# Seven products of halves instead of eight in the first matrix product of an attention and feed-forward kernel

## The chip, the cores and the metric

The kernel runs on one core of one Trainium2 chip. The metric is device microseconds of one execution, as the median of several runs. The rows of the profile come from one profiled execution; its times are in microseconds (us) from the span's start unless they say ns.

## What is computed

The inputs are q, k and v of shape (8 batches, 8 heads, 576 positions, 64), and two weights, w_in (512 x 2048) and w_out (2048 x 512). Attention is done within chunks of 64 positions, and its output goes through a feed-forward layer:

```python
scores = scale * np.matmul(q_c, k_c.transpose(0, 1, 2, 4, 3))
attn = softmax(scores)
x = np.matmul(attn, v_c)        # as 4608 tokens x 512
h = x @ w_in                    # first product, 512 -> 2048
g = np.where(h > 0.0, h, np.exp(np.minimum(h, 0.0)) - 1.0)
out = g @ w_out                 # second product, 2048 -> 512
```

All of it is in float32, the weights arrive as float64 and are turned into float32 on the chip.

## The kernel before

The 4608 tokens are worked through in 9 blocks of 512 (`TB`). The 2048 hidden features are 16 slices of 128 (index `f`), and the 512 model features are 4 slices of 128 (`kt`). A matrix is held as a sum of two float32r parts, hi and lo, and each product is made of three matmuls: hi by hi, hi by lo, lo by hi (`three`, L395). One matmul has a 128 x 128 weight operand and 512 moving columns.

For each block and each f, `hidden` (L400) makes h, 128 features x 512 tokens, with 4 x 3 matmuls that accumulate in one PSUM bank. `elu` (L408) has five operations on it: ScalarE takes the negative part (L411) and its exponential (L412), VectorE combines it with h from PSUM (L414), ScalarE casts the result to the hi part `ghi` (L419), VectorE subtracts to get `glo` (L422). `project` (L425) adds g's slice, one f later (`LAG`), to four PSUM banks `o`, one for each 128 tokens, with 4 x 3 matmuls of 512 columns. After the last f of a block `store` (L431) copies the four banks out and writes them to DRAM. All hi and lo parts of both weights stay in SBUF: `weights` (L79) holds for each half of f the tiles `wi_hi`, `wi_lo` (4096 words for each partition and tile) and `wo_hi`, `wo_lo`. In the first block they are split as they arrive.

Attention for the next block runs beside this, one tile of 128 tokens for four f (`attention_tile`, L339). Its steps are, in order: two transposes of q and k on VectorE (L275, L278), eight score matmuls (L349, two instructions each), maximum and subtraction on VectorE (L355, L369), the exponential on ScalarE (L373), the sum and the scaling on VectorE (L375 to L308), eight transfers between partitions on the DMA queue of SyncE (L320), two transposes on VectorE (L325), eight matmuls with v (L333), and a copy to `xf` on ScalarE (L384). At a block's end `split_next` (L535) makes `xhi` and `xlo` of `xf`.

PE, ScalarE, VectorE and SyncE each run their instructions in the order in which the program issues them. That order is written out by hand: a line of letters for each f (`SECOND_BLOCK` L467, `LATER` L473). H is `hidden`, P is `project` of the slice before, e is one step of `elu`, a and n are one step of the present and the next attention tile, X is `split_next`:

```python
    LATER = (
        "a a H e e e e P",
        "a H e e e e P",
        "n n H e e e e P",
        "n a a n H n X P e e e e",
    )
```

GpSimd sets constants at the start and does nothing later. SyncE issues all transfers.

Of the kernel before, what the change touches and what calls it, by code (L numbers as in the profile page):

```python
# [15 lines left out]
ALU = mybir.AluOpType  # L16
# [4 lines left out]
def kernel(  # L21
# [14 lines left out]

    nc = tc.nc
# [14 lines left out]
    Q = 32  # L52
    LAG = 1
# [13 lines left out]
    ps_h = ctx.enter_context(tc.tile_pool(name="ps_h", bufs=2, space=bass.MemoryType.PSUM))  # L67

# [158 lines left out]
    def load_tokens(n0: int):  # L227
# [4 lines left out]
        qk = stp.tile([P, STAGE], F32, name="st")  # L232
# [162 lines left out]
    def three(ps, a_hi, a_lo, b_hi, b_lo, start, stop):  # L395
        nc.tensor.matmul(ps, lhsT=a_hi, rhs=b_hi, start=start, stop=False)  # L396
        nc.tensor.matmul(ps, lhsT=a_hi, rhs=b_lo, start=False, stop=False)  # L397
        nc.tensor.matmul(ps, lhsT=a_lo, rhs=b_hi, start=False, stop=stop)  # L398
# [32 lines left out]
    def store(blk: int, o_ps):  # L431
        for tt in range(NTT):
            o = io.tile([P, DM], F32, name="q_sb" if tt % 2 else "k_sb")
            (nc.vector.tensor_copy if tt % 2 else nc.scalar.copy)(out=o, in_=o_ps[tt])
            n0 = blk * TB + tt * P
            nc.sync.dma_start(out=out[n0:n0 + P, :], in_=o)

    def warm(n: int):
# [90 lines left out]
    def project_next():  # L529
        pf, pb, po = pending.pop(0)  # L530
        project(pf, *acts.pop((pb, pf)), po)
        if pf == NF - 1:
            store(pb, po)

    def split_next():  # L535
        for kt in range(NK):
            split_x((slice(None), kt), xf[:, kt, :])

# [9 lines left out]
    def later_loads(n: int):  # L548
        return load_tokens(n * P), load_heads(v, "v_sb", n * P, io)
# [8 lines left out]
    for blk in range(NB):  # L558
        o_ps = [ps_o.tile([P, DM], F32, name=f"o{tt}") for tt in range(NTT)]
        for f in range(NF):  # L560
            tt, st = divmod(f, 4)
            n = (blk + 1) * NTT + tt + 1
            if st == 0:
                if (blk, tt) == (1, 0):
                    following = later_tile(2 * NTT, *loaded)
                tile_now, following, begun = following, iter(()), 0
                if blk > 0 and n < NB * NTT:
                    following = later_tile(n, *later_loads(n))
            lines = FIRST_BLOCK if blk == 0 else SECOND_BLOCK if (blk, tt) == (1, 0) else LATER
            for item in lines[st].split():  # L570
                if item == "H":
                    if blk == 0:
                        split_upto(f)
                        if f == NF - 1:
# [51 lines left out]
```

## Time and profile before

| | |
|---|---|
| time, median of 3 runs | 903.75 us (902.62 to 904.49) |
| the profiled execution's own time | 904.57 us |
| its span, first to last instruction | 902.8 us |
| PE busy | 886.2 us, 98% |
| weight loads (PEld) busy | 726.9 us, 81% |
| VectorE (DVE) busy | 523.6 us, 58% |
| ScalarE (ACT) busy | 409.5 us, 45% |
| GpSimd (POOL) busy | 6.1 us, 1% |
| DMA | 77.37 MB, mean 86 GB/s |

A matmul's row begins when its instruction starts and its end is modelled, so matmuls overlap in the rows: the distance of two starts is what one costs, the duration is not. A matmul that has to wait for its weights shows a longer duration. A weight load has rows of its own under PEld. An idle time in brackets is that of the engine just before the instruction, with what ended it. The granted clock is that of TensorE as a share of full speed, 2.4 GHz.

### The profile page before, as it was taken

How to read it: one execution, taken by the hardware profiler on the slowest of the kernel's cores; microseconds unless marked ns; L12 is line 12 of the kernel's file. 1: busy time of each engine (PE TensorE's matmuls, PEld its weight loads, DVE VectorE, ACT ScalarE, POOL GpSimd, SP SyncE). 2: the span in 40 equal slices, each digit the busy share in tenths (PEclk: the TensorE clock that was granted, in tenths of full speed). 3: DMA queues.
4: the chain of work that ended last, by engine and by line, in shares of the span. 5: the costliest groups of instructions: out<-in, count | busy, mean ns of one | idle time of the engine just before them, and what ended most of it. 6: DMA issues, size and time to landing. Idle time of an engine off the chain costs nothing.

```text
span 902.8 us, 12407 instructions
## 1 busy us (share of the span) xinstructions
PE 886.2 (98%) x4862; PEld 726.9 (81%) x4862; DVE 523.6 (58%) x777; ACT 409.5 (45%) x713; POOL 6.1 (1%) x12
## 2 busy tenths in 40 slices
PE   6899999999999999999999999999999999999998
PEld 6688887888888888888888878888788888888886
DVE  5789878555655565556655665456555755543222
ACT  5799984333433343334333433334333433343332
POOL 2000000000000000000000000000000000000000
PEclk9899999999999999999999999999999999999999
DMA  7775553322332224222322232222322242001001
GB/s 197 199 247 179 187 135 98 79 70 66 103 89 58 55 53 115 68 68 66 117 70 71 70 111 65 70 70 84 76 71 58 63 114 67 10 11 47 1 1 46
DMA packets 113930, 77.37 MB, mean 86 GB/s; under 512 B 63184, under 2 KB 107216, under 8 KB 113872
## 3 DMA queue, kind: packets, MB, share of 16 engines
q1 hardware_dynamic: 113872, 76.59, 30.3%
q8 instruction: 38, 0.62, 0.3%
q14 instruction: 20, 0.16, 0.1%
HBM read 59.77 MB, written 9.44 MB: 77 GB/s over the span
## 4 chain that ended last, share of the span: by engine, by line
PE 84%; DVE 4%; DMA 4%; SPq 4%; ACT 2%; issue 1%; DVEq 0%; ACTq 0%
PE h L396 13%; PE h L398 13%; PE h L397 13%; PE o L396 13%; PE o L398 13%; PE o L397 13%; PE ps_a L349 3%; PE ps_a L333 3%; DMA st<-in_moe_w_out_dram 2%; SPq L320 2%; DMA y<-y 1%; SPq L221 1%; DVE e L414 1%; DVE k_apart L278 1%; ACT ghi L419 1%
## 5 line engine op out<-in xcount | busy, mean ns | idle before, releaser
L396 PE MATMUL h<-xhi,wi_hi 128*128 128x512 f32 x576 | 228.2, 396 | 0.0
L396 PE MATMUL o<-wo_hi,ghi 128*128 128x512 f32 x576 | 225.9, 392 | 0.0
L397 PE MATMUL h<-xlo,wi_hi 128*128 128x512 f32 x576 | 225.3, 391 | 0.0
L398 PE MATMUL h<-xhi,wi_lo 128*128 128x512 f32 x576 | 225.0, 391 | 0.1
L398 PE MATMUL o<-wo_hi,glo 128*128 128x512 f32 x576 | 224.5, 390 | 0.0
L397 PE MATMUL o<-wo_lo,ghi 128*128 128x512 f32 x576 | 224.3, 389 | 0.0
L411 ACT ACTIVATE e<-h 128x512 f32<-128x512 f32 x144 | 86.1, 598 | 279.6 <-PE h L398 279.4
L414 DVE SCALAR_TENSOR_TENSOR e<-e,h 128x512 f32<-128x512 f32 x144 | 98.9, 687 | 180.6 <-ACT e L412 178.9
L422 DVE TENSOR_TENSOR glo<-e,ghi 128x512 fp32r<-128x512 f32 x144 | 99.5, 691 | 88.5 <-ACT ghi L419 87.9
L419 ACT CAST ghi<-e 128x512 fp32r<-128x512 f32 x144 | 89.3, 620 | 133.7 <-DVE e L414 133.7
L396 PEld LDWEIGHTS h<-xhi,wi_hi 128*128 128x128 f32 x576 | 108.5, 188 | 27.0 <-issue 5.2
L398 PEld LDWEIGHTS h<-xhi,wi_lo 128*128 128x128 f32 x576 | 108.5, 188 | 23.4 <-DVE wi_lo L151 0.6
L398 PEld LDWEIGHTS o<-wo_hi,glo 128*128 128x128 f32 x576 | 108.1, 188 | 23.8 <-DVE glo L422 1.2
L396 PEld LDWEIGHTS o<-wo_hi,ghi 128*128 128x128 f32 x576 | 108.1, 188 | 23.6 <-ACT ghi L419 0.8
L397 PEld LDWEIGHTS h<-xlo,wi_hi 128*128 128x128 f32 x576 | 108.5, 188 | 22.1 <-DVE xlo L391 0.6
L397 PEld LDWEIGHTS o<-wo_lo,ghi 128*128 128x128 f32 x576 | 108.1, 188 | 21.9
L412 ACT ACTIVATE e<-e 128x512 f32<-128x512 f32 x144 | 91.0, 632 | 4.6
L325 DVE STREAM_TRANSPOSE a_apart<-y 64x512 f32<-64x512 f32 x56 | 39.5, 705 | 65.5 <-DMA y<-y 63.7
L278 DVE STREAM_TRANSPOSE k_apart<-st 64x512 f32<-64x512 f32 x56 | 60.2, 1075 | 0.4
L384 ACT COPY xf<-ps_a 128x512 f32<-128x512 f32 x32 | 18.7, 584 | 42.5 <-PE ps_a L333 42.5
L349 PEld LDWEIGHTS ps_a<-k_apart,qT 128*64 128x64 f32 x512 | 27.4, 136 | 12.8 <-issue 12.8
L349 PE MATMUL ps_a<-k_apart,qT 128*64 128x128 f32 x512 | 35.0, 279 | 1.4 <-DVE k_apart L278 1.3
(55 smaller groups left out, 516.9 us busy)
## 6 DMA issues: line engine op xcount, KB each, us to landing
st<-in_q_dram SPq DMA_DIRECT2D x100, 128.0 KB, 2.7
st<-in_k_dram SPq DMA_DIRECT2D x100, 128.0 KB, 3.1
st<-in_moe_w_in_dram SPq DMA_DIRECT2D x16, 512.0 KB, 4.4
st<-in_moe_w_out_dram SPq DMA_DIRECT2D x16, 512.0 KB, 5.3
y<-y SPq DMA_DIRECT2D x224, 32.0 KB, 1.8
v_sb<-in_v_dram SPq DMA_DIRECT2D x25, 256.0 KB, 2.8
out_dram<-k_sb SPq DMA_DIRECT2D x18, 256.0 KB, 2.4
out_dram<-q_sb SPq DMA_DIRECT2D x18, 256.0 KB, 2.4
```

The source lines that it names most:

```text
L278: nc.vector.transpose(out=kbd[js, :, j, :].rearrange("p h (t u) -> p h u t", u=4), in_=qk[js, 1])
L325: nc.vector.transpose(out=a_apart[cs, :, cs].rearrange("p h (u t) -> p h u t", u=2), in_=aq[cs].rearrange("p u h k -> p h u k"),)
L333: nc.tensor.matmul(x_ps[j * D:(j + 1) * D, hp, :], lhsT=v_sb[:, h, :], rhs=a_apart[:, h, :], start=True, stop=True,)
L349: nc.tensor.matmul(s_ps[cs, 2 * hp:2 * hp + 2, :], lhsT=qT[:, hp, cs], rhs=kbd[:, hp, :, cs], start=True, stop=True,)
L396: nc.tensor.matmul(ps, lhsT=a_hi, rhs=b_hi, start=start, stop=False)
L397: nc.tensor.matmul(ps, lhsT=a_hi, rhs=b_lo, start=False, stop=False)
L398: nc.tensor.matmul(ps, lhsT=a_lo, rhs=b_hi, start=False, stop=stop)
L411: nc.scalar.activation(out=e, in_=h, func=AF.Relu, scale=-1.0)
L412: nc.scalar.activation(out=e, in_=e, func=AF.Exp, scale=-1.0)
L414: nc.vector.scalar_tensor_tensor(out=e, in0=e, scalar=-1.0, in1=h, op0=ALU.add, op1=ALU.max)
L419: nc.scalar.copy(out=ghi, in_=e)
L422: nc.vector.tensor_tensor(out=glo, in0=e, in1=ghi.bitcast(F32), op=ALU.subtract)
```

## The change

The first two blocks stay as they are, but for the order of the attention steps. From the third block on, the f are taken in pairs (56 pairs `g`: 7 blocks of 8). The product of a pair, 256 hidden features by 512 model features by 512 tokens, is cut in halves in all three directions. Seven products of halves with sums of the operands (`PRODUCTS`), each of 2 x 3 matmuls with 256 moving columns, replace eight. Two PSUM tiles of 256 columns, x and y, take them; ScalarE copies x out between them (`keep`) and VectorE adds the copies to y (`add`). Their results lie in SBUF, `straight` (elu steps A) and `cross` (elu steps B), and the elu reads them there. The subtraction for `glo` goes from VectorE to GpSimd.

In the second block `combine` makes on GpSimd the sums of the weight's halves, splits them (one copy on ScalarE, one subtraction on GpSimd), and writes all seven operands of each of the 8 pairs to a DRAM buffer `a_dram`: for each pair and partition 2 x 1792 words. From then on each pair's operands are read from there in four transfers, two pairs ahead, into three of the four `wi` tiles; the fourth holds sums of the tokens' halves. `prepare_x` makes those for each block with subtractions on VectorE, a cast each on ScalarE and a subtraction each on GpSimd, in place of `split_next`.

In the lines of order, p and a number is a product, c `keep`, d `add`, Q a quarter of a second product (3 matmuls of 512 columns; seven of a pair's eight quarters run in the next pair, the last one after that), A and B one elu step, w one of the four operand transfers, x one step of `prepare_x`, L the loads of an attention tile.

```diff
+    PRODUCTS = {1: ("A11", "B11"), 2: ("A12", "B21"), 3: ("S4", "B22"), 4: ("A22", "T4"),
+                5: ("S1", "T1"), 6: ("S2", "T2"), 7: ("S3", "T3")}
...
+        def sums(g):
...
+            for i in range(2):
+                whi, wlo = w_in_slices(2 * g + i)
+                pool(w[:, 4 * i:4 * i + 4], whi.bitcast(F32), wlo.bitcast(F32), ALU.add)
+            a11, a12, a21, a22 = [w[:, 2 * i:2 * i + 2] for i in range(4)]
+            s1, s2, s4, s3 = [s[:, 2 * i:2 * i + 2] for i in range(4)]
+            pool(s1, a21, a22, ALU.add)
+            pool(s2, s1, a11, ALU.subtract)
+            pool(s4, a12, s2, ALU.subtract)
+            pool(s3, a11, a21, ALU.subtract)
+            for lo in range(2):
...
+                nc.sync.dma_start(out=rows(g, lo)[:, :4], in_=w1.bitcast(F32))
+                nc.sync.dma_start(out=rows(g, lo)[:, 4:6], in_=w2[:, 2:].bitcast(F32))
...
+        def split(g, st):
+            nc.scalar.copy(out=st[:, 0], in_=st[:, 1].bitcast(F32))
+            pool(st[:, 1], st[:, 1].bitcast(F32), st[:, 0].bitcast(F32), ALU.subtract)
+        def write(g, st):
+            for lo in range(2):
+                nc.sync.dma_start(out=rows(g, lo)[:, 6:], in_=st[:, lo].bitcast(F32))
...
+    def load_operands(g: int):
+        buf, src = place(g % 3), a_dram[g % NG]
+        for i in range(4):
+            part = slice(i * HALF // 2, (i + 1) * HALF // 2)
+            nc.sync.dma_start(out=buf[:, part].bitcast(F32), in_=src[:, part])
+            yield
...
+        def product(self, i: int):
+            out = self.y if i in (2, 5, 3) else self.x
...
+            for k in range(2):
+                three(out, ah[:, k, :], al[:, k, :], bh[:, k, :], bl[:, k, :],
+                      i in (1, 2, 5) and k == 0, k == 1, onto=i not in (1, 2, 5))
+        def keep(self, i: int):
+            out = self.cross[:, :T2] if i == 4 else self.kept[i - 1]
+            nc.scalar.copy(out=out, in_=self.x)
+        def add(self, i: int):
+            out, kept = {1: (self.straight[:, :T2], 0), 2: (self.straight[:, T2:], 2),
+                         3: (self.cross[:, T2:], 1)}[i]
+            nc.vector.tensor_tensor(out=out, in0=self.y, in1=self.kept[kept], op=ALU.add)
...
+            nc.gpsimd.tensor_tensor(out=glo, in0=e, in1=ghi.bitcast(F32), op=ALU.subtract)
...
     LATER = (
-        "a a H e e e e P",
+        "H e e e e P",
...
+    PAIRS = (
+        "p1 c1 Q p2 d1 w x B Q x p6 c2 B Q B p5 w n n Q p7 c3 d2 A w a Q Q p4 c4 A w Q p3 d3 A A Q B",
+        "n a a L p1 c1 Q p2 d1 w B Q p6 c2 B Q B n n p5 w Q n p7 c3 d2 A n Q Q p4 c4 A w Q p3 d3 A A "
+        "Q B w",
+    )
+    LAST_PAIR = (
+        "n a a L p1 c1 x x Q p2 d1 w B Q B x p6 c2 B Q n n x p5 w x Q n p7 c3 d2 A n Q Q p4 c4 x A w "
+        "Q p3 d3 A A Q B w"
+    )
+    LAST_STEP = "n a a n H n x x x P e x e e x e"
+    FIRST_PAIR = (
+        "p1 c1 p2 d1 w a a Q p6 c2 Q x p5 w x n n Q p7 c3 d2 w A Q a x p4 c4 A w p3 d3 A A B"
+    )
```

## Rows read from the trace of the kernel before

**Rows 1.** The page: busy time of the engines, the granted clock in 40 slices.

```profile
PE 886.2 (98%) x4862; PEld 726.9 (81%) x4862; DVE 523.6 (58%) x777; ACT 409.5 (45%) x713; POOL 6.1 (1%) x12
...
PEclk9899999999999999999999999999999999999999
```

**Rows 2.** Busy time by stretch: length, engines with instructions, granted clock, DMA share, GB/s.

```profile
39.00:41.00 2.00, 2.00 (x6) 1.54 (x5) 2.00 (x4) 1.96 (x5) 0.00 (x0) 0.50 1.12 252
...
47.00:49.00 2.00, 2.00 (x13) 1.68 (x12) 1.29 (x2) 0.74 (x2) 0.00 (x0) 1.00 1.05 387
...
200.00:300.00 100.00, 100.00 (x556) 82.29 (x555) 58.54 (x87) 39.30 (x66) 0.00 (x0) 1.00 0.28 75
100.00:200.00 100.00, 99.35 (x565) 80.93 (x564) 71.53 (x106) 55.14 (x103) 0.00 (x0) 1.00 0.38 107
```

**Rows 3.** Instruction groups by form, a weight load: busy us, mean ns, idle before.

```profile
L396 PEld LDWEIGHTS h<-xhi,wi_hi 128*128 128x128 f32 x576 | 108.5, 188 | 27.0 <-issue 5.2
```

**Rows 4.** Timeline of PE: first projection matmul of two successive slices (start, duration).

```profile
876.45 0.39 PE L396 MATMUL o<-wo_hi,ghi 128*128 128x512 f32 x1
...
881.89 0.39 PE L396 MATMUL o<-wo_hi,ghi 128*128 128x512 f32 x1
```

**Rows 5.** Timeline of PE and PEld after an attention tile's matmuls, 299 to 301 us.

```profile
299.79 0.50 PE L396 MATMUL h<-xhi,wi_hi 128*128 128x512 f32 x1
299.90 0.19 PEld L397 LDWEIGHTS h<-xlo,wi_hi 128*128 128x128 f32 x1
...
300.13 0.40 PE L397 MATMUL h<-xlo,wi_hi 128*128 128x512 f32 x1
```

**Rows 6.** Timeline of PE at half the clock.

```profile
39.31 0.63 PE L398 MATMUL h<-xhi,wi_lo 128*128 128x512 f32 x1
...
40.59 0.63 PE L398 MATMUL h<-xhi,wi_lo 128*128 128x512 f32 x1
```

**Rows 7.** Timeline of PE, transposes of 128 columns; their weight loads by form.

```profile
15.03 0.60 PE L257 MATMUL ps_a<-ident,k_sb 128*128 128x128 f32 x4
15.47 0.60 PE L288 MATMUL ps_a<-ident,a 128*128 128x128 f32 x4
...
L257 PEld LDWEIGHTS ps_a<-ident,k_sb 128*128 128x128 f32 x32 | 4.1, 151 | 0.5 <-issue 0.5
```

**Rows 8.** Instruction groups by form, ScalarE and VectorE.

```profile
L414 DVE SCALAR_TENSOR_TENSOR e<-e,h 128x512 f32<-128x512 f32 x144 | 98.9, 687 | 180.6 <-ACT e L412 178.9
L412 ACT ACTIVATE e<-e 128x512 f32<-128x512 f32 x144 | 91.0, 632 | 4.6
L419 ACT CAST ghi<-e 128x512 fp32r<-128x512 f32 x144 | 89.3, 620 | 133.7 <-DVE e L414 133.7
L411 ACT ACTIVATE e<-h 128x512 f32<-128x512 f32 x144 | 86.1, 598 | 279.6 <-PE h L398 279.4
L278 DVE STREAM_TRANSPOSE k_apart<-st 64x512 f32<-64x512 f32 x56 | 60.2, 1075 | 0.4
...
L384 ACT COPY xf<-ps_a 128x512 f32<-128x512 f32 x32 | 18.7, 584 | 42.5 <-PE ps_a L333 42.5
L363 ACT ACTIVATE a<-ps_a,mx 128x64 f32<-128x64 f32 x32 | 9.5, 322 | 2.6 <-DVE mx L360 2.6
```

**Rows 9.** Timeline: the last matmul of h, and the first elu step on it.

```profile
302.42 0.39 PE L398 MATMUL h<-xhi,wi_lo 128*128 128x512 f32 x1
...
302.84 0.60 ACT L411 ACTIVATE e<-h 128x512 f32<-128x512 f32 x1 [1.72 <-PE h L398]
```

**Rows 10.** Instruction groups by form, GpSimd.

```profile
L556 POOL MEMSET a_apart<- 128x1024 f32 x1 | 1.0, 952 | 0.0
masks.py:199 POOL TENSOR_SCALAR_AFFINE_SELECT ident<-ident 128x128 f32<-128x128 f32 x1 | 0.3, 292 | 0.0
```

**Rows 11.** Timeline of SyncE's queue: the eight transfers between partitions of one tile.

```profile
284.11 4.94 SPq L320 DMA_DIRECT2D y<-y  x8
```

**Rows 12.** Timeline of PEld in the last slice's second product.

```profile
896.38 0.19 PEld L398 LDWEIGHTS o<-wo_hi,glo 128*128 128x128 f32 x1 [0.43 <-DVE glo L422]
```

More of the change, by code (lines that the diff above doesn't have):

```diff
@@ L429, in project, with store @@
             three(o_ps[tt], ghi[:, ts], glo[:, ts], hi, lo, f == 0, f == NF - 1)
-    def store(blk: int, o_ps):
-        for tt in range(NTT):
-            o = io.tile([P, DM], F32, name="q_sb" if tt % 2 else "k_sb")
+            yield
+    def store(blk: int, o_ps, tts):
+        for tt in tts:
+            if blk < PLAIN - 1:
+                o = io.tile([P, DM], F32, name="q_sb" if tt % 2 else "k_sb")
+            elif tt < NTT // 2:
+                o = gp.tile([P, DM], F32, name="o", tag="ghi" if tt % 2 else "glo")
+            else:
+                o = io.tile([P, DM], F32, name="k_sb")
             (nc.vector.tensor_copy if tt % 2 else nc.scalar.copy)(out=o, in_=o_ps[tt])
@@ new lines, in prepare_x, with minus, split, t_tile @@
+    def prepare_x():
+        b11, b12, b21, b22 = [
+            xf[:, 2 * k:2 * k + 2, t * T2:(t + 1) * T2] for k in range(2) for t in range(2)]
+        def minus(out, a, b):
+            nc.vector.tensor_tensor(out=out, in0=a, in1=b, op=ALU.subtract)
+        def split(name, src, engine):
+            hi, lo = b_operand(name)
+            nc.scalar.copy(out=hi, in_=src)
+            engine.tensor_tensor(out=lo, in0=src, in1=hi.bitcast(F32), op=ALU.subtract)
+        def t_tile(pool, tag):
+            return pool.tile([P, 2, T2], F32, name="t", tag=tag)
+        split("B11", b11, nc.gpsimd)
+        yield
+        t1, t2, t4 = t_tile(wst, "y"), t_tile(io, "q_sb"), t_tile(io, "q_sb")
+        minus(t1, b12, b11)
+        minus(t2, b22, t1)
+        minus(t4, b21, t2)
+        yield
+        split("B21", b21, nc.gpsimd)
+        yield
+        split("T2", t2, nc.gpsimd)
+        yield
+        split("T1", t1, nc.gpsimd)
+        yield
+        t3 = t_tile(io, "q_sb")
+        minus(t3, b22, b12)
+        split("T3", t3, nc.gpsimd)
+        yield
+        split("T4", t4, nc.gpsimd)
+        yield
+        split("B22", b22, nc.gpsimd)
+        yield
@@ L530, in project_next @@
         pf, pb, po = pending.pop(0)
-        project(pf, *acts.pop((pb, pf)), po)
-        if pf == NF - 1:
-            store(pb, po)
+        for tt, _ in enumerate(project(pf, *acts.pop((pb, pf)), po)):
+            if pf == NF - 1 and pb == PLAIN - 1:
+                store(pb, po, [tt])
+                yield
+        if pf == NF - 1 and pb < PLAIN - 1:
+            store(pb, po, range(NTT))
     def split_next():
@@ L537, in split_next @@
             split_x((slice(None), kt), xf[:, kt, :])
+    loads, combining, preparing, pair, kept_st = {}, combine(), iter(()), None, []
+    upcoming, second_products = None, []
     def early_tile(n: int):
@@ L559 @@
         o_ps = [ps_o.tile([P, DM], F32, name=f"o{tt}") for tt in range(NTT)]
-        for f in range(NF):
+        if blk == PLAIN:
+            x_ps, y_ps = [ps_h.tile([P, T2], F32, name="h") for _ in range(2)]
+        for f in range(0, NF, 1 if blk < PLAIN else 2):
             tt, st = divmod(f, 4)
@@ L601 @@
+    for _ in second_products[0]:
+        pass
+    for _ in pair.parts["B"]:
+        pass
+    for _ in pair.second:
+        pass
 _INS = ['q', 'k', 'v', 'moe_w_in', 'moe_w_out']
```

232 lines of the change are left out of this document (193 added, 39 removed), and 2 rows, old and new, of the table SECOND_BLOCK.

## The prediction

> **What bounds the kernel now.** I read the page first: PE is busy 98% of the span at the full clock in nearly every slice, VectorE 58%, ScalarE 45%, GpSimd almost never [rows 1]. The stretches then show where: from 200 to 300 us PE has no idle time at all [rows 2]. So what PE is given to do sets the time, and the question is what one matmul costs. The groups by form can't tell: they give durations, 188 ns for a weight load [rows 3], and loads and matmuls overlap. The timeline can: 24 matmuls lie between 876.45 and 881.89, 5.44/24 = 0.2267 us each, each with its own weight load [rows 4]. The load is hidden: where it is not, after an attention tile, the next start comes 300.13 - 299.79 = 0.34 us later, so a load that nothing covers costs 0.34 - 0.227 = 0.113 us, and the next load starts just then, at 299.90 [rows 5].
>
> **The products.** A pair's first product is now 24 matmuls of 512 columns, 5.44 us. It becomes 7 x 6 = 42 matmuls of 256 columns, and each still loads 128 x 128 weights. What such a matmul costs is in no row, and all hangs on it; 5.44/42 = 0.1295 us is where the gain is gone. From below: 256 columns at 2.4 GHz are 0.107 us. A transposition of 128 columns, with a 128 x 128 load, steps at (15.47 - 15.03)/4 = 0.110 us although its load shows 151 ns [rows 7]; so a load's duration overstates what it holds up, there by 0.041. From above, then: 0.188 - 0.041 = 0.147 us, and 0.188 at the very most. Nearest are the rows of the same operands: the exposed load, 0.113 [rows 5], and half of the 512-column step, 0.1134. Load and stream would be just as long as each other, so either one's excess shows. At half the clock the step is (40.59 - 39.31)/3 = 0.427 us, which is 512 columns at 1.2 GHz with nothing added [rows 2, 6]; at full clock it is 0.0134 above 512/2.4 = 0.2133. If this excess goes with the columns, the step is 0.1134; if it belongs to each load and matmul, 0.107 + 0.0134 = 0.120. I take 0.117, between them: 42 x 0.117 = 4.91 us, 0.53 less for a pair, and 56 x 0.526 = **29.5 us** less in all. The ends: 56 x (5.44 - 42 x 0.107) = 53 us gain, 56 x (42 x 0.147 - 5.44) = 41 us loss.
>
> **The second products and attention** keep their matmuls (24 of 512 columns a pair; the same tile steps), 5.44 us a pair and the tiles' own time, nothing saved. A product is thus always followed by a quarter of 3 x 0.227 = 0.68 us; a product takes 6 x 0.117 = 0.70.
>
> **The copies, adds and elu** move no PE work, but PE waits if they are late. A copy of 256 columns on ScalarE lies between the 64-column and the 512-column rows, 322 and 584 ns: 0.43 by proportion. An add of 256 on VectorE is under the 687 ns of 512; I take 0.43 too [rows 8]. From PE's end to ScalarE's start I count 0.2: the last matmul of h starts at 302.42, streams 0.227, and L411 starts at 302.84 [rows 9]. The tightest copy is c1, which p6 needs, since it stands behind B's two activations: after p3, 0.2 + 0.43 + 0.60 + 0.63 + 0.43 = 2.3 us; between p3 and p6 PE has Q p1 Q p2 Q, 3.4 us. Cover 1.1 us. VectorE's longest block, the next tile's three transposes (3 x 1.08 = 3.2 us [rows 8]), stands before d2, and p3, which needs d2, comes 4 us after p5. `glo` leaves this engine and three adds come, so its load stays about even.
>
> **`glo` on GpSimd** is an operation that no row shows. GpSimd writes 1024 columns in 952 ns and one-input 128 columns in 292 [rows 10]: for 512 columns 0.5 us from below and 4 x 0.292 = 1.17, or twice that with two inputs, from above. I take 1.17. What it may cost: B's chain after p6 is 0.2 + 0.43 (c2) + 0.62 (cast) + 1.17 = 2.4 us, and PE wants `glo` in the third matmul of Q6, after Q p5 Q p7 Q and two matmuls, 3.9 us later. A's chain after p7 is 0.2 + 0.43 + 0.43 + 0.60 + 0.63 + 0.69 + 0.62 + 1.17 and some 0.1 between them, 5.3 us, against 6.6. About 1.4 us of cover in both: nothing lost as long as it takes under 2.5 us. The Trainium skill (GPSIMD Engine Reference, Elementwise, side by side) gives 4497 ns for 2048 columns of two inputs, an estimate of 1.1 us for 512; the sum would be the same.
>
> **Operands from DRAM.** A pair loads 2 x 1792 words of 4 bytes by 128 partitions, 1.83 MB, in at least 10.4 us: 176 GB/s on top of 75, against 387 in the busiest stretch [rows 2]. The last of its four transfers is asked for a whole pair, over 10 us, before its own pair begins. On SyncE's queue four issues a pair stand behind a tile's eight of 4.94 us [rows 11], 0.6 each: 25 issues in two pairs (8 loads of q and k, v, these 8, 8 of operands), some 15 of 21 us. Nothing lost; if it is late, p1 of the pair after next waits.
>
> **The second block** gets, for each of 8 pairs, five times 512 columns on GpSimd, 5.9 us, a copy of 1024 on ScalarE (1.2), and six writes. They have 1.5 f or 9 us; ScalarE is 55% busy there and PE's work is untouched [rows 2]. The copy waits for GpSimd up to 2.5 us in every second pair, and the next `elu` starts late by less than the one f that lies before its use. 0 to 5 us; I take 0.5.
>
> **The seams.** Into the first pair, PE goes from H through P, 2.7 us, while four splits are made in turn on ScalarE (0.62) and GpSimd (1.17): the second one's lo part comes at about 4.0 us, p2 wants it at 3.5, and the slice's `glo` comes behind them: 1 us. At the end six quarters, 4.1 us, lie beside B's last chain of 5.5 us; the old end waited 0.43 there [rows 12]. Another 0.6 after the difference. The stores follow their quarters as before.
>
> **Sum.** The profiled execution took 904.57 us, 1.8 outside its span. 904.6 - 29.5 + 0.5 + 1.0 + 0.6 = 877.2. The median lies 0.8 below this execution, within what the sum can tell: **877**.
>
> **Rivals.**
> 1. *The weight load becomes the bound, and it is slower.* The place is each of the 2352 half matmuls. If the next load can't start until the last is wholly in, the step is the shown 0.188: 42 x 0.188 = 7.90 us, +2.46 a pair, +137.5 in all, 1044 us with the seams; at 0.147, 948. It decides from 0.1295 on. Against: the load beside a matmul lasts as long as the bare one, and the bare one holds its matmul up 0.113 only [rows 5]. For: two steps as long as each other leave no slack. 11%.
> 2. *Loads do not overlap at all with a matmul on the same rows of the array*: step 0.113 + 0.113 = 0.227, 42 x 0.227 = 9.53 us, +4.09 a pair, 229 in all, 1136 us. The Trainium skill (TensorE: Matmul & The Clock Gate, Part 3, The mechanism) says that a weight load overlaps with running matmuls only where the row group differs, and all rows are used here. By that rule the trace should show 0.340 for every matmul; it shows 0.227 with a load in each [rows 4, 5], and disagrees. 1%.
> 3. *GpSimd is the new wait.* Where `glo` takes over 2.5 us, PE waits twice a pair; from 2.8 on it eats the 0.48 us a pair that are left, and at 3.5 it is 2 us a pair, some 990 us. VectorE's combination now reads two SBUF operands beside it. The Trainium skill (SBUF, two separate sides) has GpSimd and such an operation exclude each other for a whole instruction; 0.69 in front of 1.17 would still be 1.9, under 2.5. No row has the two together. 5%.
> 4. *Small waits in the chain*, 0.2 to 0.45 us a pair, where each product must hear from ScalarE, GpSimd and a transfer: +11 to +25, 888 to 902 us. 13%; to the point of no difference, 4%.
> 5. *The half matmuls cost 0.107 to 0.112*: 854 to 866 us. 8%.
> 6. The forecast, 0.112 to 0.122 and seams up to a few us: 866 to 890. 58%.
>
> **How the numbers follow.** Slower are 1 to 3, 17%; the same, which is within 0.2% or what a measurement of this kernel can tell, 4%; faster the rest, 79%. The range takes in case 6, 4, and the upper half of 5, from 861 to 902, about 8 in 10.
>
> **What would show it.** In the changed profile: product starts 0.113 to 0.120 apart; PE without idle time in the third to last block; `glo` on GpSimd near 1.2 us; the four operand transfers landing a pair early; the second block as long as before. Starts over 0.13 apart make the prediction wrong in sign; PE idle after GpSimd or ScalarE makes it wrong in size.

## The result

The changed kernel takes 907.08 us (median of 10 runs, 905.94 to 910.37), the kernel before 903.4 us in the same comparison (902.5 to 904.76): a ratio of 1.0045, 95% interval [1.0033, 1.0057]. It is slower by 0.45%, where 877 us was forecast.

The profiled execution took 905.94 us, its span 904.1. The page of the kernel after, engines and granted clock, beside [rows 1]:

```profile
PE 874.0 (97%) x5870; PEld 752.6 (83%) x5870; DVE 537.4 (59%) x833; ACT 497.3 (55%) x966; POOL 285.4 (32%) x229
...
PEclk9999999999999999999999999999999999999999
```

PE is busy 12 us less than before, and the span is 1.3 us longer: what the fewer products gained went into idle time of PE. The second block, from the start of its first slice's product to that of its last, shows the same by stretch (length, engines with instructions, clock, DMA share, GB/s). Kernel before:

```profile
135.96:228.15 92.19, 91.54 (x505) 74.76 (x503) 57.16 (x85) 33.78 (x56) 0.00 (x0) 1.00 0.28 78
```

Kernel after:

```profile
133.86:233.95 100.09, 93.25 (x506) 74.39 (x504) 64.55 (x86) 40.65 (x64) 61.39 (x51) 1.00 0.72 233
```

From 200 to 300 us, where the kernel before had no idle time on PE [rows 2], the one after has 8.3 us (PE busy is the second figure):

```profile
200.00:300.00 100.00, 91.68 (x580) 77.22 (x581) 59.38 (x90) 45.63 (x85) 37.35 (x30) 0.98 0.84 264
```

What a pair costs undisturbed is read from the first of its four copies by ScalarE, c1, to the next pair's c1. The last block has no attention beside it; every fourth copy of the timeline of ScalarE:

```profile
842.05 0.36 ACT L613 COPY kept<-h 128x256 f32<-128x256 f32 x1
...
852.59 0.36 ACT L613 COPY kept<-h 128x256 f32<-128x256 f32 x1
...
863.13 0.36 ACT L613 COPY kept<-h 128x256 f32<-128x256 f32 x1
```

It is 10.54 us, against 2 x 5.44 = 10.88 [rows 4]: 0.34 us gained a pair, where 0.526 was forecast. Two pairs with an attention tile take 23.17 us everywhere. At the end of a block they don't. Here c1 of a block's last pair starts at 515.06, c1 of the next block's first pair at 528.16, and that of its second pair at 540.21:

```profile
515.06 0.38 ACT L613 COPY kept<-h 128x256 f32<-128x256 f32 x1 [0.31 <-PE h L406]
...
528.16 0.36 ACT L613 COPY kept<-h 128x256 f32<-128x256 f32 x1
...
540.21 0.37 ACT L613 COPY kept<-h 128x256 f32<-128x256 f32 x1 [0.31 <-PE h L406]
```

13.10 + 12.05 = 25.15, so each of the six seams between two blocks of pairs loses 2.0 us. The sum of the forecast, with what each term turned out to be:

| term | forecast, us | measured, us |
|---|---|---|
| 56 pairs | -29.5 | 56 x -0.34 = -19.0 |
| second block | +0.5 | 100.09 - 92.19 = +7.9 |
| first pair of the third block | +1.0 | +6.7 |
| six seams between blocks | 0 | 6 x 2.0 = +12.0 |
| the end | +0.6 | -0.2 |
| start of the program, waits of the kernel before, rest | 0 | -6.1 |
| sum, from 904.6 | 877.2 | 905.9 |

The first pair is read from the starts of products on PE: from p1 of the first pair (239.52) to p1 of the third (265.87) 26.35 us pass. Two ordinary pairs take 23.17; five of their quarters fall to the end of the program here (5 x 0.70 = 3.5), so 19.7 were due, and 6.7 are lost. The last line before the sum holds three things. The second block begins 2.1 us earlier than before; but in nine of the kernels run here, with the same first block, it begins anywhere from 133.9 to 136.0 us, so this is no doing of the change. In blocks six and seven 2.3 us come back where the kernel before had waited itself (97.1 and 96.3 us a block, 95.5 in the others before them). The remaining 1.7 were not traced.

### The profile page after: what moved, and what is told of

It reads as the page before. It is cut to its first block, busy times and chain, and to the rows that moved or that the text cites. A ratio compares the mean times of both kernels' runs of the same rounds, so it can differ in the third digit from the quotient of the medians.

```text
span 904.1 us, 15897 instructions
## 1 busy us (share of the span) xinstructions
PE 874.0 (97%) x5870; PEld 752.6 (83%) x5870; DVE 537.4 (59%) x833; ACT 497.3 (55%) x966; POOL 285.4 (32%) x229
## 4 chain that ended last, share of the span: by engine, by line
PE 73%; DVE 7%; ACT 5%; issue 4%; DMA 4%; POOL 3%; SPq 3%; POOLq 0%; ACTq 0%; DVEq 0%
PE o L406 34%; PE h L406 32%; PE ps_a L357 3%; PE ps_a L341 2%; POOL st L481 2%; DMA wi_hi<-a_dram 1%; DVE t L554 1%; DVE y L316 1%; DMA q_sb<-in_q_dram 1%; SPq L247 1%; POOL wi_lo L632 1%; ACT wi_hi L630 1%; DMA wi_lo<-a_dram 1%; DVE z L383 1%; PE ps_a L265 1%
## 5 line engine op out<-in xcount | busy, mean ns | idle before, releaser
L632 POOL TENSOR_TENSOR wi_lo<-e,wi_hi 128x512 fp32r<-128x512 f32 x112 | 144.9, 1294 | 418.2 <-ACT wi_hi L630 418.2
L406 PE MATMUL h<-xhi,wi_hi 128*128 128x256 f32 (+1 forms) x720 | 182.5, 305 | 1.9 <-ACT xhi L558 1.3
L406 PE MATMUL o<-wo_lo,wi_hi 128*128 128x512 f32 x448 | 177.6, 397 | 0.0
L406 PE MATMUL o<-wo_hi,wi_hi 128*128 128x512 f32 x448 | 177.4, 396 | 0.0
L406 PE MATMUL o<-wo_hi,wi_lo 128*128 128x512 f32 x448 | 175.2, 391 | 2.0 <-POOL wi_lo L632 1.6
L406 PEld LDWEIGHTS h<-xhi,wi_hi 128*128 128x128 f32 x720 | 125.3, 189 | 19.7 <-issue 3.2
L406 PE MATMUL h<-xlo,wi_hi 128*128 128x256 f32 (+1 forms) x424 | 133.7, 315 | 2.0 <-DVE xlo L399 1.1
L406 PE MATMUL h<-xhi,wi_lo 128*128 128x256 f32 (+1 forms) x432 | 118.1, 318 | 0.4 <-DVE kept L618 0.4
L406 PEld LDWEIGHTS h<-wi_lo,wi_hi 128*128 128x128 f32 x666 | 94.0, 189 | 14.8 <-ACT kept L613 3.6
L406 PE MATMUL h<-wi_lo,wi_hi 128*128 128x256 f32 x666 | 97.8, 282 | 3.4 <-ACT kept L613 1.7
L406 PEld LDWEIGHTS o<-wo_lo,wi_hi 128*128 128x128 f32 x448 | 85.6, 191 | 2.6
```

Of the source, the lines that this page charges most:

```text
L406: nc.tensor.matmul(ps, lhsT=a, rhs=b, start=start, stop=stop, skip_group_check=onto)
L632: nc.gpsimd.tensor_tensor(out=glo, in0=e, in1=ghi.bitcast(F32), op=ALU.subtract)
```

## The experiments

Each kernel is the changed one with the edit shown, unless it says another base. The ratio is to the kernel before, run beside it.

**What a half matmul costs.** (`p1_five`) The first product of every second pair is made five times.

```diff
-        "p1 c1 Q p2 d1 w x B Q x p6 c2 B Q B p5 w n n Q p7 c3 d2 A w a Q Q p4 c4 A w Q p3 d3 A A Q B",
+        "p1 p1 p1 p1 p1 c1 Q p2 d1 w x B Q x p6 c2 B Q B p5 w n n Q p7 c3 d2 A w a Q Q p4 c4 A w Q p3 d3 A A Q B",
```

> In every other ordinary pair the first product is made five times over (the first four results are overwritten), so 30 half matmuls of 256 columns run in a row, with no quarter between. Theory: a half matmul costs 0.120 to 0.122 us (half of the full stream at 2.4 GHz, 0.107, and what each load and matmul adds), and the 0.1175 us that the records show beside the quarters is the same cost, with a part of it shown in the quarter behind it; then the starts in the long row settle at 0.120 or more. Rival: the half matmul costs 0.1175 and the quarters are slow for a reason of their own; then the starts in the row stay at 0.1175.

The one run took 982.02 us. Two pairs take 26.05 us in place of 23.17: 2.88/24 = 0.120 us for each added half matmul. Timeline of PE within the five products:

```profile
453.15 0.40 PE L406 MATMUL h<-xhi,wi_lo 128*128 128x256 f32 x2
453.39 0.28 PE L406 MATMUL h<-xlo,wi_lo 128*128 128x256 f32 x1
453.51 0.40 PE L406 MATMUL h<-xhi,wi_lo 128*128 128x256 f32 x2
...
456.38 0.28 PE L406 MATMUL h<-xhi,wi_lo 128*128 128x256 f32 x1
```

The starts are 0.120 apart, (456.38 - 453.15)/27. With 0.2267 for 512 columns [rows 4], 256 columns more cost 0.1067, which is 256 at 2.4 GHz: the excess, 0.0134, belongs to each load and matmul and not to the columns (how it is shared between the load and the matmul, two sizes can't tell). In the changed kernel itself a product shows 0.71 us and the quarter behind it 0.70 and not 0.68, so the part of the excess that the product's starts hide (0.1175 apart) is paid in the quarter. Timeline of PE, first of a product, first of a quarter, first of the next product:

```profile
500.11 0.28 PE L406 MATMUL h<-xhi,wi_hi 128*128 128x256 f32 x1
...
500.82 0.40 PE L406 MATMUL o<-wo_hi,wi_hi 128*128 128x512 f32 x1
...
501.52 0.28 PE L406 MATMUL h<-xhi,wi_lo 128*128 128x256 f32 x1
```

**Fewer changes between the two sizes.** (`in_twos`) Two products in a row, then two quarters.

```diff
-        "p1 c1 Q p2 d1 w x B Q x p6 c2 B Q B p5 w n n Q p7 c3 d2 A w a Q Q p4 c4 A w Q p3 d3 A A Q B",
-        "n a a L p1 c1 Q p2 d1 w B Q p6 c2 B Q B n n p5 w Q n p7 c3 d2 A n Q Q p4 c4 A w Q p3 d3 A A "
+        "p1 c1 p2 d1 Q w x B Q x p6 c2 B B p5 Q w n n Q p7 c3 d2 A w a Q Q p4 c4 A w p3 d3 Q A A Q B",
+        "n a a L p1 c1 p2 d1 Q w B Q p6 c2 B B n n p5 Q w Q n p7 c3 d2 A n Q Q p4 c4 A w p3 d3 Q A A "
```

> Two products follow each other in three places of each ordinary pair, with two quarters behind them, instead of one by one. In the changed kernel a product and a quarter cost 0.705 us each, where the quarter should be 0.680. Theory: the excess belongs to each change from 256 to 512 columns, so fewer changes make a pair cheaper by about 0.08 us, 10.46 us in the last block and 902 to 904 us in all. Rival: it belongs to the steps themselves and nothing changes in a pair; or the shorter distance brings waits for ScalarE's copies, and it is slower.

907.95 us, ratio 1.0041 [1.0026, 1.0056]; a pair without attention takes 10.56 us. Two products now take 1.43 us, two quarters 1.39:

```profile
850.69 0.88 PE L406 MATMUL h<-wi_lo,wi_hi 128*128 128x256 f32 x6
...
852.12 0.40 PE L406 MATMUL o<-wo_hi,wi_hi 128*128 128x512 f32 x1
...
853.51 0.28 PE L406 MATMUL h<-xhi,wi_lo 128*128 128x256 f32 x1
```

The pair stays the same, so the loss isn't tied to the changes from one size to the other, as my theory had it (10.46 us); it sits in the matmuls.

**Whose queue is short at the seam.** (`x_on_dve`) The seven subtractions of `prepare_x` go from GpSimd to VectorE.

```diff
-        split("B11", b11, nc.gpsimd)
+        split("B11", b11, nc.vector)
...
```

> The seven subtractions of prepare_x go back to VectorE; all else as in the changed kernel (907.1 us). Theory: in the last pair of each block (2.0 us lost at each of six seams) GpSimd is the cause. Its subtractions stand in front of glo and hold up VectorE's operations with two SBUF operands (the three subtractions for T1, T2, T4 took 3.1 us instead of 2.07, the scaling of the attention weights up to 1.5 instead of 0.69). Then the seams lose 0.7 us or less each, the first pair 1 to 3 us less, and the time is 895 to 900 us. Rival: VectorE's and ScalarE's queues are simply too full there; seven times 0.69 us more on VectorE leaves the seams at 2 us or makes them longer, 905 to 915 us.

937.07 us, ratio 1.0362 [1.0346, 1.0378]. Ordinary pairs stay at 23.17, the last pair of a block goes from 13.1 to 18.4 us. My theory fell: VectorE has no room at the seam for seven operations more. That GpSimd has no part in it is not shown, since in most blocks the first pair of the next one gets 0.67 us shorter (11.38 for 12.05). In the changed kernel the timeline of VectorE in a last pair shows what stands in the way: two subtractions for the tokens' differences, 1.2 us each, and the scaling of the attention, 1.50 (0.69 us is the least that each of these takes). They stand in front of two adds, d1 at 517.83, which B's step behind it needs, and d2 at 523.88, which PE waits for:

```profile
515.51 2.39 DVE L554 TENSOR_TENSOR t<-xf,t 128x512 f32<-128x512 f32 x2
517.83 0.41 DVE L618 TENSOR_TENSOR kept<-h,kept 128x256 f32<-128x256 f32 x1
...
522.46 1.50 DVE L316 TENSOR_TENSOR y<-a,z 128x512 f32<-128x512 f32 x1
523.88 0.41 DVE L618 TENSOR_TENSOR kept<-h,kept 128x256 f32<-128x256 f32 x1
```

PE's waits follow, first for a copy that stands behind the delayed B step on ScalarE, then for d2, then for a `glo` that stands behind a subtraction on GpSimd (timeline of PE; by the distances of starts these three cost some 0.7, 0.4 and 0.6 of the 2.0 us):

```profile
520.39 0.98 PE L406 MATMUL h<-wi_lo,wi_hi 128*128 128x256 f32 x6 [0.42 <-ACT kept L613]
524.34 0.38 PE L406 MATMUL h<-xhi,wi_hi 128*128 128x256 f32 x1 [0.18 <-DVE kept L618]
529.14 0.50 PE L406 MATMUL o<-wo_hi,wi_lo 128*128 128x512 f32 x1 [0.30 <-POOL wi_lo L632]
```

**`glo` back on VectorE.** (`glo_on_dve`)

```diff
-            nc.gpsimd.tensor_tensor(out=glo, in0=e, in1=ghi.bitcast(F32), op=ALU.subtract)
+            nc.vector.tensor_tensor(out=glo, in0=e, in1=ghi.bitcast(F32), op=ALU.subtract)
```

> Only the subtraction for glo in the pairs goes back to VectorE. Theory: the undisturbed pairs are bound by PE, so a pair without attention stays at 10.54 us, and only the seams get shorter, by the wait for glo behind T3's subtraction (0.3 to 0.5 us each): 903 to 907 us. Rival: glo on GpSimd (1.29 us) holds every pair back a little; then the undisturbed pair gets shorter by over 0.1 us and the time falls to 900 us or less.

932.9 us, ratio 1.032 [1.0303, 1.0338]. Pairs without attention stay at 10.54, two pairs with it take 23.96, a last pair 15.1. The move to GpSimd costs an ordinary pair nothing, as the theory had it, but the seams got longer here and not shorter: the move is needed, since VectorE has no room for `glo` beside the attention.

**The seam in another order.** (`seam_order`) The T4 difference is made later and in place, the x steps of the last pair and of the first one are moved.

```diff
-        minus(t4, b21, t2)
...
-        split("T4", t4, nc.gpsimd)
+        minus(t2, b21, t2)
+        split("T4", t2, nc.gpsimd)
...
-        "n a a L p1 c1 x x Q p2 d1 w B Q B x p6 c2 B Q n n x p5 w x Q n p7 c3 d2 A n Q Q p4 c4 x A w "
-        "Q p3 d3 A A Q B w"
+        "n a a L p1 c1 x x Q p2 d1 w B Q x p6 c2 B B Q n n x p5 w x Q p7 c3 d2 n A n Q Q p4 c4 A w "
+        "Q p3 d3 A A x Q B w"
...
-        "p1 c1 p2 d1 w a a Q p6 c2 Q x p5 w x n n Q p7 c3 d2 w A Q a x p4 c4 A w p3 d3 A A B"
+        "p1 c1 x p2 d1 x w a a Q p6 c2 Q x p5 w n n Q p7 c3 d2 w A Q a p4 c4 A w p3 d3 A A B"
```

> The same operations in another order in the last pair of a block and in the first pair of all. Last pair: c2 ahead of the cast for B, the scaling step of the attention tile behind d2, T3's split behind the glo of A, T4's sum one pair later (in place of T2's buffer). First pair: the steps for T3, T4 and B22 a quarter or two earlier. Theory: the 2.0 us of a seam and some 6 us of the first pair are waits behind other work in the in-order queues of VectorE, ScalarE and GpSimd, which x_on_dve made longer by 5.3 us a seam. Then order alone takes most of it away: a seam loses under 0.8 us, the first copy of the third block to that of the second pair is 3 us or more shorter, and the time is 893 to 899 us. Rival: the seam is short of VectorE time, not of order; the waits move to other places and the time stays at 904 us or more.

905.59 us, ratio 1.0000 [0.9987, 1.0013], where 893 to 899 was expected. Last pair and next first one take 24.4 us: 1.2 us lost in each seam in place of 2.0. This is not order alone. In the new order VectorE's subtractions for the differences and its scaling no longer run beside GpSimd's, and each is as short as alone: from 257 us on the scaling takes 692 ns in the mean (866 in the changed kernel), the second kind of subtraction 686 (1179). The first pair of the third block stays at 16.33. What is left in it stands in the timeline of PE:

```profile
254.72 0.39 PE L406 MATMUL h<-xhi,wi_hi 128*128 128x256 f32 x1 [3.17 <-DVE kept L618]
257.89 1.09 PE L341 MATMUL ps_a<-a_apart,v_sb 128*64 128x128 f32 x16 [1.17 <-issue]
```

and at a seam in that of GpSimd, where `glo` (L632), which PE waits 0.64 us for, stands behind two subtractions of `prepare_x`:

```profile
437.18 1.31 POOL L559 TENSOR_TENSOR wi_lo<-t,wi_lo 128x512 fp32r<-128x512 f32 x1 [1.50 <-ACT wi_lo L558]
438.44 1.29 POOL L559 TENSOR_TENSOR xlo<-xf,xhi 128x512 fp32r<-128x512 f32 x1
439.69 1.28 POOL L632 TENSOR_TENSOR wi_lo<-e,wi_hi 128x512 fp32r<-128x512 f32 x1
```

**These two as well.** (`seam2`) On the last kernel, T4 and B22 are moved behind B's last step, and in the first pair the transposes behind the add.

```diff
-        "p1 c1 Q p2 d1 w x B Q x p6 c2 B Q B p5 w n n Q p7 c3 d2 A w a Q Q p4 c4 A w Q p3 d3 A A Q B",
+        "p1 c1 Q p2 d1 w B Q p6 c2 B Q B x p5 w n n Q x p7 c3 d2 A w a Q Q p4 c4 A w Q p3 d3 A A Q B",
...
-        "p1 c1 x p2 d1 x w a a Q p6 c2 Q x p5 w n n Q p7 c3 d2 w A Q a p4 c4 A w p3 d3 A A B"
+        "p1 c1 x p2 d1 x w a a Q p6 c2 Q x p5 w Q p7 c3 d2 w A n n Q a p4 c4 A w p3 d3 A A B"
```

> The kernel of seam_order with two more moves at the seams: in the first pair of a block T4 and B22 are made after B's last step and not ahead of it, and in the first pair of the third block the next tile's transposes stand behind the first two steps of A. Nothing is left out. Theory: what seam_order left of the seam (1.2 us in each of six) is GpSimd's glo standing behind the subtractions of T4 and B22, and 3.2 us of the first pair are the add d2 standing behind the transposes on VectorE. Then the last pair and the first of the next block take 23.2 to 23.8 us together where they took 24.4, the first pair 14 to 15 us where it took 16.3, and the run is 899 to 902 us, ratio 0.994 to 0.997. Rival: the later T4 and B22 only move the wait to p4 and p3, and A's combination behind the transposes to the first quarter of the next pair; then both distances stay and the run is at 904 to 906.

900.89 us, ratio 0.9974 [0.9963, 0.9984]: faster than both kernels. Last and first pair take 12.25 + 11.23 = 23.48, 0.3 us over two ordinary ones, as expected. The first pair does not gain, 17.08 (14 to 15 was expected): PE now waits 2.05 us for the transposes of k, and 2.06 ahead of the matmuls with v, where a transpose on VectorE has waited for the tile's transfers. There the waits moved on, as the rival had it.

**The second block without the sums.** (`no_sums`) The sums, the copies on ScalarE and the splits on GpSimd are left out, and plain weights written in their place, so the products from the third block on are of other operands. As many bytes are written, but in eight transfers for each pair where the changed kernel has six.

```diff
-                pool(w[:, 4 * i:4 * i + 4], whi.bitcast(F32), wlo.bitcast(F32), ALU.add)
...
-            nc.scalar.copy(out=st[:, 0], in_=st[:, 1].bitcast(F32))
-            pool(st[:, 1], st[:, 1].bitcast(F32), st[:, 0].bitcast(F32), ALU.subtract)
+            pass
...
-                nc.sync.dma_start(out=rows(g, lo)[:, 6:], in_=st[:, lo].bitcast(F32))
+                for i in range(2):
...
+                    nc.sync.dma_start(out=rows(g, lo)[:, 6 + 4 * i:10 + 4 * i], in_=w.bitcast(F32))
```

> Leaves out the sums of the weights' halves, their copies on ScalarE and their splits on GpSimd in the second block; the transfers to DRAM keep their size and take the plain weights instead, so the pairs multiply by other numbers. Theory: the second block is 7.9 us longer (100.1 instead of 92.2 us from its first to its sixteenth slice) because ScalarE's copy waits in order for GpSimd and holds up the elu behind it. Then that stretch is 92 to 93 us and the time 898 to 900 us. Rival: it is the 14.7 MB of writes on SyncE's queue or the moved attention steps; then the stretch stays at 97 us or more.

904.73 us, ratio 1.0004 [0.9994, 1.0014]; the stretch of the second block 98.54 us. All its steps, from one slice's first product to the next one's, are as in the kernel before, but for the last: 13.76 us where the kernel before took 7.43, a stall of 6.3 us (and not of 8.3, as a later expectation has it). So all five steps that were longer in the changed kernel (by 1.0, 1.1, 1.6, 0.7 and 3.5 us) had to do with the sums and splits. In the last two of them, 4.2 us, PE waits for ScalarE; the changed kernel's timelines show it, GpSimd first, then ScalarE:

```profile
210.96 2.40 POOL L481 TENSOR_TENSOR st<-st 128x1024 fp32r<-128x1024 f32 x1 [1.16 <-ACT st L506]
213.31 2.99 POOL L481 TENSOR_TENSOR st<-wi_hi,wi_lo 128x512 f32<-128x512 f32 x2
216.38 3.38 POOL L481 TENSOR_TENSOR st<-st 128x256 f32<-128x256 f32 x4
```

```profile
219.79 1.05 ACT L506 CAST st<-st 128x1024 fp32r<-128x1024 f32 x1 [5.37 <-POOL st L481]
220.74 0.59 ACT L423 ACTIVATE e<-h 128x512 f32<-128x512 f32 x1
```

The copy holds ScalarE 5.37 us for GpSimd's sums, the first `elu` step stands behind it, and PE waits 2.93 us for `ghi` at 223.42. In the first three of the five, 3.7 us, PE waits for VectorE instead: 0.83 us for `xlo` at 135.08, 0.55 and 1.31 for transposes of k at 153.28 and 204.00, 1.11 for one of y at 155.48 (0.65 before).

Without the sums another queue comes to light. `y` is ready on VectorE at 211.03, and SyncE issues its transfers five us later, behind transfers of weights; timeline of SyncE, then of VectorE:

```profile
214.46 1.51 SPq L518 DMA_DIRECT2D wi_hi<-a_dram  x1
216.07 4.95 SPq L328 DMA_DIRECT2D y<-y  x8
```

```profile
210.34 0.69 DVE L316 TENSOR_TENSOR y<-a,z 128x512 f32<-128x512 f32 x1
...
221.53 1.52 DVE L333 STREAM_TRANSPOSE a_apart<-y 64x512 f32<-64x512 f32 x2 [6.83 <-DMA y<-y]
```

The changed kernel doesn't have this delay: its `y` is ready only at 217.66, and SyncE, done with its weights since 215.73, issues the transfers at 217.68. How late they would be there without the sums is not shown, as this run has two transfers more for each pair in that queue.

**Both queues, first try.** (`block2`) The split comes a slice later, and the four plain transfers of a pair are issued from ScalarE's queue.

```diff
-                nc.sync.dma_start(out=rows(g, lo)[:, :4], in_=w1.bitcast(F32))
+                nc.scalar.dma_start(out=rows(g, lo)[:, :4], in_=w1.bitcast(F32))
...
```

> In the second block alone: ScalarE's copy for the split comes two thirds of a step later, so that GpSimd has made its sums by then, and the four transfers of plain operands for each pair are issued by ScalarE's queue instead of SyncE's. Theory: the stretch of 100.1 us has two causes that cover each other, ScalarE waiting in order for GpSimd, and SyncE's queue being full so that the attention transfers (y) are issued 5 us late; no_sums took away the first alone and got 98.5 us. With both gone it is 92.5 to 94.5 us and the time 900 to 903 us. Rival: GpSimd's use of VectorE's port or the traffic itself is what costs; then it stays at 97 us or more.

913.46 us, ratio 1.0107 [1.0069, 1.0145], the stretch 107.8 us. Issued there, the transfers stand in ScalarE's own queue: four issues last from 211.47 to 216.68, and the next copy starts at 216.72. Waits from 134 to 250 us that ended with such an issue (engine, line, what for: us, times, longest):

```profile
ACT st L506 <- DMA a_dram<-wi_lo: 4.7, 1, 4.7
ACT xf L392 <- DMA a_dram<-wi_hi: 4.6, 1, 4.6
```

PE's longest wait in this stretch, 3.52 us at 210.85, is for transposes of k on VectorE. How much of the 107.8 us the issues cost is therefore not shown.

**Both queues, second try.** (`block2b`) The plain transfers are issued in the first block; one of two additions goes to VectorE; GpSimd makes the next sums ahead of the last split.

```diff
-            for i in range(2):
+            for i, add in ((1, nc.vector.tensor_tensor), (0, nc.gpsimd.tensor_tensor)):
...
+                if blk == 0 and f >= NF - NG:
+                    write_plain(f - (NF - NG))
```

> The changed kernel with another second block alone: the copies of the plain weight operands to DRAM (4 transfers a pair) are issued in the second half of the first block, one of the two additions of hi and lo goes to VectorE, the sums of the next pair stand ahead of the split of the last one on GpSimd, and the writes go in the middle of a slice. Nothing is left out. Theory: the 7.9 us that the second block lost are two queues, ScalarE's copy standing behind GpSimd's sums (by GpSimd's 8.5 us a pair in 8.2) and SyncE's queue, which has some 25 us of issues in 24 us there, so that y's transfers start 5 us late. Then the stretch from the 1st to the 16th slice of the second block falls from 100.1 to 92 to 95 us and the run to 900 to 903 us, ratio 0.994 to 0.998. Rival: it is the traffic itself (a DMA share of 0.91 from 210 to 235 us) or operations on VectorE and GpSimd that hold each other up; then the stretch stays at 98 or more and the run at 906 to 908.

917.3 us, ratio 1.0148 [1.0135, 1.0162], the stretch 106.83. One step of it takes 19.08 us; VectorE's timeline has the reason, an addition into a buffer that a late write still reads, with the rest of VectorE's work behind it:

```profile
207.65 0.69 DVE L498 TENSOR_TENSOR st<-wi_hi,wi_lo 128x512 f32<-128x512 f32 x1 [8.44 <-DMA a_dram<-st]
```

The same on top of seam2 (`all2`):

> block2b and seam2 together. Nothing is left out. If the losses are separate queues in separate stretches they add up: 907.1 less 5 for the second block, 1.5 for seam_order, 5 for the seams left, 895 us, ratio 0.988 to 0.992, faster than both kernels by over 0.8%; what is left against the forecast of 877 is then the half matmul alone, 56 times the 0.19 us by which a pair's gain was over-sized, some 10 us, and a seam at the start and the end. Rival: the gains overlap or the stalls move on to the next queue; then the run is at 900 or above.

909.93 us, ratio 1.0064 [1.0051, 1.0078]; its step took 20.22 us. The gains at the seams stayed.

**Third try** (`all3`), on seam2: the last two pairs' sums and splits later, so that no engine waits for that buffer.

```diff
+        summed, parted, written = (
+            (0, 1, 3, 4, 6, 7, 10, 11), (1, 2, 4, 5, 7, 8, 12, 13), (3, 3, 6, 6, 9, 9, 14, 14))
```

> seam2 with another second block: as in block2b, but the sums and splits of the last two pairs come one to four slices later, and pair 6 makes both of its additions on GpSimd. Nothing is left out. block2b kept every step of the second block as before but one, where VectorE stood 8.4 us for a buffer that a write to DRAM still read. Theory: with that wait gone nothing but the two queues had cost the second block its 7.9 us; then its stretch is 93 to 96 us where seam2 took 100.3, no step is over 9.5 us, and the run 894 to 898 us, ratio 0.989 to 0.994. Rival: the wait moves on again, to ScalarE behind the later sums or to SyncE behind the later writes; then one step of slices 10 to 15 is over 10 us and the run at 899 or above.

897.97 us, ratio 0.9938 [0.9927, 0.9950], the fastest of all. The stretch of the second block:

```profile
135.20:230.23 95.03, 91.98 (x506) 74.78 (x504) 65.23 (x91) 41.29 (x64) 54.97 (x48) 1.00 0.48 158
```

No step is over 9.05 us. The first pair behind it takes 19.03 us, 2 more than in seam2, and eats part of this gain. PE stands idle longer there, and its granted clock is 0.76 over the pair, where it was 0.85: an estimate of 19.03 x 0.24 = 4.6 us lost by the clock, against 17.08 x 0.15 = 2.6.

**SyncE's part alone** (`early`), on seam2.

```diff
+                if blk == 0 and f >= NF - NG:
+                    write_plain(f - (NF - NG))
```

> seam2 with SyncE's part of the second block alone: the 32 transfers of the plain weight operands to DRAM are issued in the second half of the first block; sums, splits and writes stay where the change has them. Nothing is left out. all3, which moved both, took the stretch of the second block from 100.3 us to 95.0; the run without the sums and splits alone left one stall of 8.3 us behind SyncE's queue. If each of the two queues costs a stall of its own at another place, this run keeps the steps of about 9 us where ScalarE's copy stands behind GpSimd (slices 10 and 13), and its stretch is 97 to 100 us. If SyncE's backlog is the cause of ScalarE's waits too (GpSimd waiting for a buffer that a late write still reads), the stretch falls to 95 or less and the run to 896 to 898 us. If neither, over 100.

900.4 us, ratio 0.9963 [0.9947, 0.9978], the same as seam2, and the stretch is no shorter (seven kernels with the changed kernel's second block took from 100.1 to 102.6 us for it):

```profile
134.16:234.92 100.76, 94.47 (x505) 75.45 (x503) 63.71 (x85) 40.59 (x64) 63.94 (x54) 0.98 0.51 173
```

ScalarE still waits 4.61 and 5.36 us for GpSimd, so SyncE's backlog is not what makes it wait. The stretch is 100.3 us with neither queue eased, 100.8 with SyncE's, 98.5 without the sums, 95.0 with both. That fits two stalls of which each hides the other. It doesn't show it: GpSimd's part of the third try, with SyncE's queue as it was, was not run, and the run without the sums has the longer queue on SyncE.

## Why the prediction was wrong

**What bounds the kernel** was read rightly: PE alone, so the price of a half matmul carries the gain [rows 2, 4]. Two steps failed. The larger is the cover, by which PE would wait 2.1 us in all (0.5, 1.0 and 0.6 in the sum): it waits 26.4, in the six seams (12.0, no term in the sum), the second block (7.9) and the first pair (6.7). The smaller is the price of the pairs, 10.5 us. Of the 28.7 us that the forecast missed, the waits are 24.3 and the price 10.5; 6.1 came back, as the table has it.

**The products.** The step that failed here is the choice of 0.117 between 0.1134 and 0.120: it is 0.120 in a long row, and a pair's 42 cost 42 x 0.120 = 5.04 us, 0.40 less than before and not 0.53. Undisturbed pairs show 0.34; the last 0.06 us was not traced to a row. The rows of before did not decide it: at half the clock nothing is added to 512 columns [rows 6], and nothing to 256 either, in the first pair of the third try (granted clock 0.50, ten steps of 0.213 us, which is 256 columns at 1.2 GHz; timeline of PE):

```profile
254.60 0.42 PE L406 MATMUL h<-xlo,wi_lo 128*128 128x256 f32 x1
...
256.73 0.37 PE L406 MATMUL h<-xhi,wi_lo 128*128 128x256 f32 x1
```

The Trainium skill (TensorE: Matmul & The Clock Gate, Wait — 56ns, not 53.3ns?) has a fixed cost of 2.5 ns for each matmul in a row at the full clock, whatever its columns. The runs agree that it is fixed, and differ in its size: 13.4 ns here, where each matmul has a load of its own. I had not weighed that rule. Rivals 1 and 2, a load that is the bound, did not occur.

**The second products and attention** were not untouched: "nothing saved" held, but a quarter costs 0.70 and not 0.68.

**The copies, adds and elu.** In ordinary pairs the cover held: two take 23.17 us in every block, and PE waits for nothing there. The add took 422 ns (0.43 taken), the copy 367. What failed is that the cover was worked out for an ordinary pair and then counted for all. The last pair of a block has `prepare_x` in it, four operations of 512 columns more on VectorE than an ordinary one, and I had given those no term at all: 2.0 us in each of six seams. The kernel before had four subtractions on VectorE at a block's end too, but neither the adds behind them nor GpSimd's beside them. That the loss lies in how they are arranged, and not in their number, is shown by seam2, which has all of them and loses 0.3 us. "Its load stays about even" was true as a mean (58% to 59%) and false where it decides.

**`glo` on GpSimd** takes 1.29 us, against 1.17 taken and an end of 2.3; it is hidden in an ordinary pair. GpSimd's group by form:

```profile
L632 POOL TENSOR_TENSOR wi_lo<-e,wi_hi 128x512 fp32r<-128x512 f32 x112 | 144.9, 1294 | 418.2 <-ACT wi_hi L630 418.2
```

The third rival, GpSimd as the new wait in all pairs, did not come. Rival 4, small waits in the chain, had the right kind but the wrong place: it was priced for every pair, and the waits came at the seams and in the second block alone.

**Operands from DRAM.** In the later blocks they cost nothing, as forecast. In the second block SyncE's queue had no sum of its own; the writes and the tiles' transfers fill it there, and in the run without the sums, with two transfers more for each pair, that is a stall of 6.3 us.

**The second block.** The step that failed is "five times 512 columns on GpSimd, 5.9 us": it is six times, and each longer than taken, 2 x 1.42 + 4 x 0.83 + 2.40 = 8.6 us for a pair, where 1.5 slices without attention are 8.2. GpSimd runs behind, the copy that waits for it holds ScalarE for up to 5.4 us and not 2.5, and the one slice of cover doesn't hold it. That is 4.2 of the 7.9 us lost in place of 0.5. The other 3.7 are waits for VectorE, which the sum had not looked at here: its subtraction for `glo` took 0.99 us in the mean and up to 1.75 in this block, beside GpSimd's sums, where it took 0.69 before. The third try took back some 5 of the 7.9 us.

**The seams.** The first pair was costed by `prepare_x` alone, 1.0 us; it lost 6.7. PE's four waits there are indeed for casts and subtractions of `prepare_x` (timeline of PE):

```profile
245.34 0.38 PE L406 MATMUL h<-wi_lo,wi_hi 128*128 128x256 f32 x1 [0.72 <-ACT wi_lo L558]
246.69 0.85 PE L406 MATMUL h<-wi_lo,wi_hi 128*128 128x256 f32 x5 [0.97 <-POOL wi_lo L559]
...
250.30 0.38 PE L406 MATMUL h<-xhi,wi_hi 128*128 128x256 f32 x1 [1.31 <-ACT xhi L558]
251.64 0.38 PE L406 MATMUL h<-xlo,wi_hi 128*128 128x256 f32 x1 [0.96 <-POOL xlo L559]
```

But these come late because copies of `store`, attention steps and the elu stand in front of them in VectorE's and ScalarE's queues, as the timelines have it; no run shows it, since in each try to mend this pair the waits only moved on. PE slows beside this. Its granted clock is 1.00 from 240 to 252 us, where the four waits lie, and 0.66 from 252 to 257, so part of that is at the lower level, 1.2 GHz. Over the first pair it is 0.90, an estimate of 16.35 x 0.10 = 1.6 of the 6.7 us; PE is busy 12.38 of 16.35 us:

```profile
240.58:256.93 16.35, 12.38 (x87) 10.31 (x86) 10.44 (x17) 7.73 (x16) 6.78 (x6) 0.90 0.75 237
```

The end cost nothing (-0.2), where 0.6 was taken. Slower had 17%, all of it on rivals that were priced by load or GpSimd in every pair; that gains and waits at the seams could cancel was not among the cases.

The fastest kernel is 20.8 us over the forecast: 10.5 are the pairs, some 9 the first pair, 2.3 the second block and 2 the six seams, less some 3 that come back as in the table. What the first pair would be with its transfers in time was not tried.

## What to carry to other kernels

Halving an operation that carries a fixed cost pays it twice: measure two sizes, split the time into a part by size and a fixed part, and only then count what fewer, smaller ones save. Where one engine is full and the rest have slack on average, cost the change in each distinct stretch of the schedule, with every operation that stands in the same in-order queue there; the seams and the second block, which come rarely, lost here what all the pairs gained. When easing one queue gains nothing, ease the next together with it before giving up on the cause, and each alone as well, or what the pair of them shows stays open.

## What the hardware showed beyond that

VectorE's operations on two SBUF operands got longer beside GpSimd: y (L316) from 692 to 862 ns in the mean and 1.50 us at worst, while the same engine's adds that read one operand from PSUM took 0.41 to 0.43 all through. The two subtractions at 515.51 (2.39 us) lie beside one of GpSimd's from 516.03 to 517.35. With the seven subtractions on VectorE (x_on_dve) and nothing on GpSimd beside them, the pair of them at 533.79 took 1.42 us. This agrees with the Trainium skill (SBUF — State Buffer, SBUF: two separate sides), by which such an operation and one of GpSimd exclude each other for a whole instruction; I had cited it for `glo` alone, where it did no harm, and not for `prepare_x` and the second block's sums, beside which VectorE got slower. How much of the time lost is due to this no run shows by itself; seam_order and seam2 changed order and overlap at once.

In block2 transfers issued from ScalarE's queue took 0.37 to 0.61 us each of that queue in the median (by line and source) and 2.73 at worst, one after the other, and waits of ScalarE of up to 4.7 us ended with such a transfer. What the queue waited for inside was not settled.
